# Strassen output product: stores of groups 1 to 7 issued by GpSimd behind its placing of the keys; banks of the x tiles shifted by two

## The chip, the cores and the metric

The kernel runs on one core of a Trainium2 chip. The metric is device time in microseconds, as the median of several executions. A profile is one execution recorded by the hardware profiler; times within it count from the start of its span. The engines are TensorE (PE; its weight loads are listed apart as PEld), VectorE (DVE), ScalarE (ACT), GpSimd (POOL) and SyncE (SP). A name with a small q (ACTq, SPq) is the engine's queue of instructions, where the issue of a transfer shows.

## The reference: what is computed

An attention with pooled keys and values for 8 batches of 8 heads feeds a two-layer block over all 4608 tokens.

```python
# q, k, v: (8, 8, 576, 64) float32
k_p = k.reshape(B, H, 72, 8, D).mean(axis=3)
v_p = v.reshape(B, H, 72, 8, D).mean(axis=3)
scores = matmul(q, k_p.T) / sqrt(D)
attn = softmax(scores)
x = matmul(attn, v_p)                  # -> (4608, 512), one row per token
h = x @ w_in                           # (4608, 2048)
out = (h - tanh(h)) @ w_out            # (4608, 512)
```

The kernel works through the tokens in nine groups of 512 (0 to 8). From group 1 on the last product is made with Strassen's seven half-size products instead of eight.

## The kernel before: the parts that matter here

Each group g from 1 to 8 has two stages. In the hidden stage TensorE computes 16 blocks of h, in seven pairs and two single blocks; ScalarE makes the Tanh and VectorE the difference. In the product stage the seven products run, and between them the attention of batch nb = g + 1 is made, which fills later columns of xT. Meanwhile the keys, values and queries of batch nn = g + 2 are loaded and pooled. Group 6 is the first for which there is no nn, groups 7 and 8 have no nb either.

```python
def h_pair(g, p, b0, ts):
    h_mms(g, p, PS[:, b0, :])                 # line 530: 4 multiplies each
    h_mms(g, p + NP, PS[:, b0 + 1, :])
    t2 = TS[:, 2 * ts : 2 * ts + 2, :]
    nc.scalar.activation(out=t2, in_=PS[:, b0 : b0 + 2, :], func=ACT.Tanh)            # 542
    nc.vector.tensor_sub(out=Gt[:, p, :, :], in0=PS[:, b0 : b0 + 2, :], in1=t2)       # 543
# h_one, lines 547 and 548: the same for one block

def store_tile(g, tb):
    for r0, r1, dst in out_segments(g * TG + tb * 128, 128):
        nc.scalar.dma_start(out=dst, in_=O[r0:r1, tb, :])                             # 607
# out_segments: one piece of 128 rows or two of 64, by where the tile lies in its batch

def after_product(g, n):                      # parts of it
    if n == 0:
        nc.scalar.copy(out=m4, in_=chain(g, C1))                                      # 624
    if n == 1:
        nc.vector.tensor_tensor(out=O[:, 2:4, 0:HD], in0=chain(g, C2), in1=m4, ...)   # 626
        sum_d(0, 2); sum_d(2, 4)                                                      # 561
    if n == 2:
        nc.scalar.copy(out=m45, in_=chain(g, C1))                                     # 630
        nc.gpsimd.tensor_tensor(out=m4, in0=O[:, 2:4, 0:HD], in1=m45, ...)            # 631
        sum_d(4, 6); sum_d(6, 8)
    if n == 3:
        nc.vector.tensor_tensor(out=O[:, 0:2, HD:DM], in0=m4, in1=chain(g, C2), ...)  # 635
    ...                                       # n == 4: 637, 638; n == 5: 640

for g in range(1, NG):
    nb = g + 1 if g + 1 < B else None
    nn = g + 2 if g + 2 < B else None
    for p in range(NP - 1):                   # hidden stage
        c = p if g > 1 else p - 1
        if nb is not None and 0 <= c < 3:
            q_cast_part(nb, c)                # ScalarE, lines 192 and 197
        h_pair(g, p, (0, 2, 4, 6, 0, 2, 4)[p], p % 2)
        ...                                   # sum_p: VectorE, line 551
        if g > 1 and p >= 3:
            store_tile(g - 1, p - 3)
        if nb is not None and p == 0:
            k_dma_transpose(nb)               # SyncE, line 332
            k_place(nb, nc.gpsimd.tensor_copy)   # lines 300, 301, 304
        if nb is not None and 0 <= c < 3:
            q_dma_transpose(nb, 2 * c, min(2 * c + 2, R + 1))   # SyncE, line 205
        if nb is not None and c == 2 and nn is not None:
            load_k(nn); load_v(nn); load_q(nn)   # SyncE, lines 137, 146, 141, 170, 162
    h_one(g, NP - 1, 1, 0, 2)
    h_one(g, NP - 1, 0, 1, 3)
    ...
    ps_a = Banks(2, 3, 4, 5, 0, 1)            # each tile takes the next bank in turn
    for u in range(14):                       # product stage
        n, half = u // 2, u % 2
        product(...)                          # line 586
        if half:
            after_product(g, n)
        if nb is not None:
            if u < NT:                        # NT = 5
                scores(nb, u)                 # two tiles of ps_a; Exp: line 368
            if u in (6, 7, 8, 9, 11):
                av(nb, (6, 7, 8, 9, 11).index(u), ps_b1, True)   # two tiles of ps_a
            if u == 6 and nn is not None:     # lines 248 to 256 and 267 to 291
                pool_k(nn, nc.gpsimd); pool_v(nn, nc.gpsimd)
    if g < NG - 1:
        nc.scalar.copy(out=O[:, 0:2, 0:HD], in_=chain(g, C1))    # line 980
```

The function av multiplies the exponentials with the values (line 396), divides on VectorE (lines 413 and 414, output x_sb) and lets SyncE transpose the result into xT by a transfer (line 434). O is a single buffer of one group's output: it is rewritten in the product stage while its earlier contents were stored in the hidden stage.

Of the kernel before, what the change touches and what calls it, by code (L numbers as in the profile page):

```python
# [28 lines left out]
NT = 5  # L29
# [13 lines left out]
def kernel(  # L43
# [9 lines left out]
    nc = tc.nc  # L53
# [30 lines left out]
    ps_a = Banks(5, 6, 7)  # L84
# [19 lines left out]
    O = const.tile([128, 4, DM], FP32, name="O")  # L104
# [45 lines left out]
    def load_k(b):  # L150
        return [
            load_main(k_pairs, k_raw[b % 2], b, 0, NM),
            load_dense(k_pairs, k_raw[b % 2], b),
        ]

    def load_v(b):
        return [load_main(v_pairs, v_raw[b % 2], b, 0, NM)] + load_left(
            v_pairs, v_raw[b % 2], b
        )
# [29 lines left out]
    def q_cast_part(b, n):  # L189
        t = q_raws[b]  # L190
        if n < 2:
            nc.scalar.copy(
                out=q_bf[:, 2 * n : 2 * n + 2, :, :].rearrange("p j h d -> p h j d"),
                in_=t[:, :, 2 * n : 2 * n + 2, :],
            )
        else:
            nc.scalar.copy(out=q_bf[:QT, R, :, :], in_=q_raws.pop(b)[:QT, :, R, :])

    def q_dma_transpose(b, j0=0, j1=R + 1):
        if j0 == 0:  # L200
            qTs[b] = work.tile([128, NHP, S], BF16, name="qT", tag="qT")
        qT = qTs[b]
        for j in range(j0, j1):
            rows = 128 if j < R else QT
            nc.sync.dma_start_transpose(  # L205
                out=qT[:, :, j * 128 : j * 128 + rows],
                in_=q_bf[:rows, j, :, :].rearrange("p h d -> p (h d)"),
            )
# [89 lines left out]
    def kb_main(kb, ps, t0, t1, engs):  # L298
        kv = kb.rearrange("p (t x) -> p t x", x=KP)
        engs[0](out=kv[0:D, t0:t1, 0:G], in_=ps[0:D, :, 0:G])  # L300
        engs[1](out=kv[D:128, t0:t1, G:128], in_=ps[D:128, :, G:128])

    def kb_left(kb, ps, eng):
        eng(
            out=kb[D:128, :].rearrange("p (t x) -> p t x", x=KP)[:, :, 128 : 128 + LO],
            in_=ps[D:128, 0 : NM * LO].rearrange("p (x t) -> p t x", t=NM),
        )
# [22 lines left out]
    def k_dma_transpose(b):  # L330
        kT = work.tile([128, NT, 128], BF16, name="kT", tag="kT", bufs=1)
        nc.sync.dma_start_transpose(
            out=kT[:, :, :], in_=kdups.pop(b)[:, :, :, :].rearrange("p t a d -> p (t a d)")
        )
        kTs[b] = kT

    def k_place(b, eng):
        kT = kTs.pop(b)
        kb_main(KB[b % 2], kT[:, 0:NM, :], 0, NM, (eng, eng))
        kb_left(KB[b % 2], kT[:, NM, :], eng)  # L340
# [3 lines left out]
    def score_mms(b, t, dst, c0, c1, pairs=range(NM)):  # L344
        for m in pairs if t == NM else (t,):
            o = m * KP + (128 if t == NM else 0)
            w = 32 if t == NM else 128
            p = 32 * m if t == NM else 0
            nc.tensor.matmul(  # L349
                dst[p : p + w],  # L350
                lhsT=KB[b % 2][:, o : o + w],
                rhs=qTs[b][:, m, c0:c1],
                start=True,
                stop=True,
            )

    def scores(b, t):
        if t == 0:
            E_tiles[b] = work.tile([128, NT, S], BF16, name="E", tag="E", bufs=1)
        E = E_tiles[b]  # L360
        hs = S // 2
        pss = []
        for half in range(2):
            ps = ps_b1([128, hs], FP32, "s_ps")
            score_mms(b, t, ps[:, :], half * hs, (half + 1) * hs)
            pss.append(ps)
        for half, ps in enumerate(pss):
            nc.scalar.activation(  # L368
                out=E[:, t, half * hs : (half + 1) * hs], in_=ps[:, :], func=ACT.Exp, scale=SCALE
            )  # L370
# [85 lines left out]
    def out_segments(c0, nrows):  # L456
        segs = []
        r = 0
        while r < nrows:
            c = c0 + r  # L460
            bb = c // S
            i = c % S
            if i < QA:
                j = i // 128
                p0 = i % 128
                ln = min(128 - p0, nrows - r, QA - i)
                dst = out[bb * S : bb * S + QA, :].rearrange("(p j) m -> p j m", j=R)[
                    p0 : p0 + ln, j, :
                ]
            else:  # L470
                ln = min(S - i, nrows - r)
                dst = out[bb * S + i : bb * S + i + ln, :]
            segs.append((r, r + ln, dst))
            r += ln
        return segs
# [62 lines left out]
    def h_pair(g, p, b0, ts):  # L538
        h_mms(g, p, PS[:, b0, :])
        h_mms(g, p + NP, PS[:, b0 + 1, :])  # L540
        t2 = TS[:, 2 * ts : 2 * ts + 2, :]
        nc.scalar.activation(out=t2, in_=PS[:, b0 : b0 + 2, :], func=ACT.Tanh)  # L542
        nc.vector.tensor_sub(out=Gt[:, p, :, :], in0=PS[:, b0 : b0 + 2, :], in1=t2)  # L543
# [6 lines left out]
    def sum_p(a, b):  # L550
        nc.vector.tensor_tensor(  # L551
            out=P[:, a:b, :], in0=Gt[:, a:b, 0, :], in1=Gt[:, a:b, 1, :], op=ALU.add
        )

    def sum_q(a, b):
        nc.vector.tensor_tensor(
            out=Q[:, a:b, :], in0=Gt[:, a:b, 0, 0:HT], in1=Gt[:, a:b, 1, HT:TG], op=ALU.add
        )
# [9 lines left out]
    def w_sum(out, a, b, op, eng=nc.vector, k0=0, k1=NP):  # L568
        return eng.tensor_tensor(  # L569
            out=out[:, k0:k1, :], in0=a[:, k0:k1, :], in1=b[:, k0:k1, :], op=op  # L570
        )
# [32 lines left out]

    def store_tile(g, tb):
        for r0, r1, dst in out_segments(g * TG + tb * 128, 128):
            nc.scalar.dma_start(out=dst, in_=O[r0:r1, tb, :])

    def sh(c, off):
        return slice(c.start + off, c.stop + off)  # L610
# [99 lines left out]
    for m, base, step, cm in (  # L710
# [6 lines left out]
            out=m,  # L717
            in_=m,
# [6 lines left out]
    for i in range(2):  # L725
# [4 lines left out]
        out=spread.rearrange("p (t x) -> p t x", x=32)[:, :, 0:LO],  # L730
        in_=ident[:, 0 : NM * LO].rearrange("p (x t) -> p t x", t=NM),
# [44 lines left out]
    def ps_b1(shape, dtype, name):  # L776
        return ps_a.tile(shape, dtype, name=name, tag="ps_a")
# [110 lines left out]
    for u in range(16):  # L888
        qd, tb = u // 4, u % 4
# [27 lines left out]
        if u in (9, 11):  # L917
            n = (u - 9) // 2
            nc.scalar.mul(
                out=w2s[:, 4, 4 * n : 4 * n + 4, :], in_=b22[:, 4 * n : 4 * n + 4, :], mul=-1.0  # L920
# [10 lines left out]
# [3 lines that stand above are left out]
        for p in range(NP - 1):  # L934
            c = p if g > 1 else p - 1
            if nb is not None and 0 <= c < 3:
                q_cast_part(nb, c)
            h_pair(g, p, (0, 2, 4, 6, 0, 2, 4)[p], p % 2)
            if g == 1 and p < 4:
                w_sum(w2s[:, 0, :, :], b11, b22, ALU.add, k0=2 * p, k1=2 * p + 2)  # L940
            if 3 <= p < 6:
                sum_p(2 * p - 6, 2 * p - 4)
            if g > 1 and p >= 3:
                store_tile(g - 1, p - 3)
            if nb is not None and p == 0:
                k_dma_transpose(nb)
                k_place(nb, nc.gpsimd.tensor_copy)
            if nb is not None and 0 <= c < 3:
                q_dma_transpose(nb, 2 * c, min(2 * c + 2, R + 1))
            if nb is not None and c == 2:  # L950
                if nn is not None:
                    load_k(nn)
                    load_v(nn)
                    load_q(nn)
        h_one(g, NP - 1, 1, 0, 2)
        h_one(g, NP - 1, 0, 1, 3)
        sum_p(6, 8)
        sum_q(0, 4)
        sum_q(4, 8)
        ps_a = Banks(2, 3, 4, 5, 0, 1)  # L960
        for u in range(14):
            n, half = u // 2, u % 2
            bk, lhs, rhs = products[n]
            if n == 6 and g == NG - 1:
                break
            product(g, bk, lhs, rhs, 4 * half, 4 * half + 4, n < 2)
            if half:
                after_product(g, n)
                if g == 1 and n in (1, 2):
                    w_sum(w2s[:, 2, :, :], b21, b22, ALU.add, k0=4 * n - 4, k1=4 * n)  # L970
            if nb is not None:
                if u < NT:
                    scores(nb, u)
                if u in (6, 7, 8, 9, 11):
                    av(nb, (6, 7, 8, 9, 11).index(u), ps_b1, True)
                if u == 6 and nn is not None:
                    pool_k(nn, nc.gpsimd)
                    pool_v(nn, nc.gpsimd)
        if g < NG - 1:
            nc.scalar.copy(out=O[:, 0:2, 0:HD], in_=chain(g, C1))  # L980
# [43 lines left out]
```

## Time and profile before

| | |
|---|---|
| time, median of 3 (range) | 326.88 us (323.62 to 327.22) |
| span of the profiled execution | 324.4 us, 5421 instructions |
| mean granted TensorE clock | 0.963 |
| busy: PE, DVE, ACT, POOL | 287.1, 229.6, 153.0, 122.7 us |
| busy: share of the span | 88%, 71%, 47%, 38% |
| moved by transfers | 49.84 MB, mean 154 GB/s |
| stores by line 607 | 44, from ScalarE: 32 of 128 KB, 12 of 256 KB, median 2.9 us to land |
| weight loads from GpSimd | 8 of 512 KB, median 13.9 and 17.0 us to land |

Busy shares are averages over stages with different limits. The hidden stage and the product stage of one group can have different bounds, and idle time of an engine that nobody waits for costs nothing. What counts is, at each stage, the wait that ends last; the timeline of a stage, beside the same stage of another group, shows it.

### The profile page before, as it was taken

The numbers are of one execution on the slowest core, as the hardware profiler recorded it, in microseconds if no ns is written. First come the engines' busy times: TensorE is split into PE (matmuls) and PEld (weight loads), VectorE is DVE, ScalarE is ACT, GpSimd is POOL, SyncE is SP. The second block draws the span as 40 slices with busy tenths as digits, with TensorE's granted clock in tenths as the row PEclk, the third lists the DMA queues.
The fourth block names the chain that finished last, engine by engine and source line by source line (L and its number), as shares of the span: only waits on it lengthen the run. The fifth ranks groups of instructions, "written<-read, shape, count | busy, mean of one in ns | idle before, by whom it ended". The sixth has DMA issues, their size and how long they took to land.

```text
span 324.4 us, 5421 instructions
## 1 busy us (share of the span) xinstructions
PE 287.1 (88%) x2021; PEld 181.2 (56%) x2040; DVE 229.6 (71%) x400; ACT 153.0 (47%) x244; POOL 122.7 (38%) x122
## 2 busy tenths in 40 slices
PE   7999999989896499989994697949999999999990
PEld 3554455448643277458642484427846864774680
DVE  5668567799864568788783396737969868947950
ACT  4566674754271433763461524545177326415410
POOL 8403649902970029605950069300980100010020
PEclk9999999999999589999999699998999999999998
DMA  8999999677358813787869603697246033101205
GB/s 262 211 236 267 300 271 313 116 238 218 65 105 244 281 43 65 126 240 264 114 143 317 201 16 60 125 316 219 49 104 146 18 58 77 55 2 61 68 2 130
DMA packets 66379, 49.84 MB, mean 154 GB/s; under 512 B 39985, under 2 KB 53297, under 8 KB 66353
## 3 DMA queue, kind: packets, MB, share of 16 engines
q1 hardware_dynamic: 54736, 35.60, 41.8%
q10 hardware_dynamic: 6864, 9.18, 9.9%
q0 software_dynamic: 4752, 4.72, 8.7%
q8 instruction: 16, 0.26, 0.4%
q14 instruction: 11, 0.08, 0.1%
HBM read 36.70 MB, written 9.44 MB: 142 GB/s over the span
## 4 chain that ended last, share of the span: by engine, by line
PE 57%; DMA 17%; DVE 10%; POOL 4%; SPq 3%; ACT 3%; issue 2%; ACTq 1%; DVEq 0%; POOLq 0%
PE PS L586 26%; PE PS L530 21%; DMA k_raw<-in_k_dram 7%; DMA w1b<-in_moe_w_in_dram 4%; DVE Gt L543 4%; PE PS L512 3%; PE PS L396 3%; PE PS L349 3%; DMA v_raw<-in_v_dram 3%; SPq L205 3%; ACT TS L542 2%; DMA qT<-q_bf 2%; DVE x_sb L414 1%; DVE w2s L569 1%; POOL k_raw L248 1%
## 5 line engine op out<-in xcount | busy, mean ns | idle before, releaser
L530 PE MATMUL PS<-xT,w1b 128*128 128x512 bf16 x496 | 111.1, 379 | 5.4 <-DVE x_sb L414 2.5
L543 DVE TENSOR_TENSOR Gt<-PS,TS 128x1024 bf16<-128x1024 f32 x56 | 68.4, 1222 | 46.9 <-ACT TS L542 46.9
L530 PEld LDWEIGHTS <-w1b 128*128 128x128 f16 x512 | 49.7, 98 | 64.2 <-issue 2.8
L542 ACT ACTIVATE TS<-PS 128x1024 f32<-128x1024 f32 x56 | 57.3, 1025 | 53.5 <-PE PS L530 26.6
L631 POOL TENSOR_TENSOR m<-O,m 128x512 f32<-128x512 f32 x8 | 11.5, 1438 | 159.9 <-ACT m L630 125.6
L586 PEld LDWEIGHTS <-Gt 128*128 128x128 bf16 x256 | 23.9, 98 | 28.3 <-DVE Gt L543 17.0
L586 PE MATMUL PS<-w2s,Gt 128*128 128x256 f16 x128 | 19.4, 286 | 20.2 <-DVE Gt L543 15.6
L414 DVE TENSOR_TENSOR x_sb<-PS,rden 128x256 bf16<-128x256 f32 x72 | 30.6, 425 | 2.5
L586 PE MATMUL PS<-w2s,Dg 128*128 128x256 f16 x256 | 30.2, 272 | 0.0
L586 PEld LDWEIGHTS <-P 128*128 128x128 bf16 x256 | 26.4, 105 | 6.7 <-issue 1.4
L248 POOL TENSOR_TENSOR k_raw<-k_raw 128x512 f32<-128x512 f32 (+2 forms) x13 | 22.5, 1746 | 16.3 <-DMA k_raw<-in_k_dram 16.3
L368 ACT ACTIVATE E<-PS 128x288 bf16<-128x288 f32 x60 | 21.4, 412 | 10.8 <-PE PS L349 10.7
L586 PEld LDWEIGHTS <-Dg 128*128 128x128 bf16 x256 | 24.6, 98 | 2.8 <-issue 0.2
L561 DVE TENSOR_TENSOR Dg<-Gt 128x1024 bf16<-128x1024 bf16 x32 | 23.2, 785 | 0.0
L551 DVE TENSOR_TENSOR P<-Gt 128x1024 bf16<-128x1024 bf16 x32 | 22.0, 687 | 0.6
L396 PE MATMUL PS<-VB,E 128*128 128x130 bf16 x240 | 20.2, 220 | 0.1
L586 PE MATMUL PS<-w2b,P 128*128 128x256 f16 x128 | 19.8, 310 | 0.0
L267 POOL TENSOR_TENSOR v_raw<-v_raw 128x512 f32<-128x512 f32 (+1 forms) x12 | 19.2, 1623 | 0.0
L349 PE MATMUL PS<-qT,KB 128*128 128x288 bf16 (+5 forms) x128 | 18.5, 303 | 0.3
L637 ACT COPY m<-PS 128x512 f32<-128x512 f32 x8 | 4.7, 587 | 29.5 <-PE PS L586 29.5
L396 PEld LDWEIGHTS <-E 128*128 128x128 bf16 x240 | 16.8, 98 | 1.9 <-issue 0.4
L586 PE MATMUL PS<-w2s,P 128*128 128x256 f16 x128 | 16.5, 275 | 0.0
(108 smaller groups left out, 371.7 us busy)
## 6 DMA issues: line engine op xcount, KB each, us to landing
k_raw<-in_k_dram SPq DMA_DIRECT2D x7, 1024.0 KB, 6.2
q_raw<-in_q_dram SPq DMA_DIRECT2D x7, 1024.0 KB, 8.2
v_raw<-in_v_dram SPq DMA_DIRECT2D x7, 1024.0 KB, 8.7
out_dram<-O ACTq DMA_DIRECT2D x32, 128.0 KB, 2.9
out_dram<-O ACTq DMA_DIRECT2D x12, 256.0 KB, 2.9
w1b<-in_moe_w_in_dram POOLq DMA_DIRECT2D x4, 512.0 KB, 13.9
w2b<-in_moe_w_out_dram POOLq DMA_DIRECT2D x4, 512.0 KB, 17.0
out_dram<-O SPq DMA_DIRECT2D x4, 256.0 KB, 5.0
```

What stands on the lines that cost most here:

```text
L248: first = eng.tensor_tensor(out=r[:, ta:tb, 0:4, :], in0=r[:, ta:tb, 0:4, :], in1=r[:, ta:tb, 4:8, :], op=ALU.add)
L267: eng.tensor_tensor(out=r[:, ta:tb, 0:4, :], in0=r[:, ta:tb, 0:4, :], in1=r[:, ta:tb, 4:8, :], op=ALU.add)
L349: nc.tensor.matmul(dst[p : p + w], lhsT=KB[b % 2][:, o : o + w], rhs=qTs[b][:, m, c0:c1], start=True, stop=True,)
L368: nc.scalar.activation(out=E[:, t, half * hs : (half + 1) * hs], in_=ps[:, :], func=ACT.Exp, scale=SCALE)
L396: nc.tensor.matmul(ps[:, 2 * n : 2 * n + 2, :].rearrange("p h d -> p (h d)") if n < 2 else ps.rearrange("p (a s) d -> p a s d", s=2)[:, :, ...
L414: nc.vector.tensor_tensor(out=x_sb[:, half, :, :], in0=ps[:, :, 0:D], in1=rden[:, :, :].to_broadcast([128, 4, D]), op=ALU.mult,)
L530: nc.tensor.matmul(dst, lhsT=w1b[:, fb, i * 128 : (i + 1) * 128], rhs=xT[:, fb, c0 : c0 + TG], start=(fb == 0), stop=(fb == NFB - 1),)
L542: nc.scalar.activation(out=t2, in_=PS[:, b0 : b0 + 2, :], func=ACT.Tanh)
L543: nc.vector.tensor_sub(out=Gt[:, p, :, :], in0=PS[:, b0 : b0 + 2, :], in1=t2)
L551: nc.vector.tensor_tensor(out=P[:, a:b, :], in0=Gt[:, a:b, 0, :], in1=Gt[:, a:b, 1, :], op=ALU.add)
L561: nc.vector.tensor_tensor(out=Dg[:, a:b, :, :], in0=Gt[:, a:b, :, 0:HT], in1=Gt[:, a:b, :, HT:TG], op=ALU.subtract,)
L586: nc.tensor.matmul(part(g, bk, tt), lhsT=lhs(k, slice(tt * 128, (tt + 1) * 128)), rhs=rhs[:, k, :], start=(first and k == 0 and (tt == 0 o ...
```

## The change

The stores of groups 1 to 7 (line 607) are issued by GpSimd instead of ScalarE, and no longer one tile after each of the hidden pairs 3 to 6 but all four tiles after the first pair, behind the placing of the keys in GpSimd's queue. The purpose is to keep store issues out of ScalarE's queue, in which the Tanh stands, without holding up the placing. Where a following batch exists, the rotation of ps_a is also advanced by two tiles between the scores and the x tiles, so that the x tiles use other banks of PSUM.

```diff
     def store_tile(g, tb):
         for r0, r1, dst in out_segments(g * TG + tb * 128, 128):
-            nc.scalar.dma_start(out=dst, in_=O[r0:r1, tb, :])
+            nc.gpsimd.dma_start(out=dst, in_=O[r0:r1, tb, :])
...
             if 3 <= p < 6:
                 sum_p(2 * p - 6, 2 * p - 4)
-            if g > 1 and p >= 3:
-                store_tile(g - 1, p - 3)
             if nb is not None and p == 0:
                 k_dma_transpose(nb)
                 k_place(nb, nc.gpsimd.tensor_copy)
+            if g > 1 and p == 0:
+                for tb in range(4):
+                    store_tile(g - 1, tb)
...
                 if u < NT:
                     scores(nb, u)
+                if u == NT:
+                    ps_a.n += 2
                 if u in (6, 7, 8, 9, 11):
                     av(nb, (6, 7, 8, 9, 11).index(u), ps_b1, True)
```

The other stores stay as they were: group 0's tiles are stored by SyncE (line 525), and group 8's by SyncE and ScalarE (lines 603 and 993).

## The prediction

> **What bounds the kernel now.** I began with the summary by engine and the chain that ended last. TensorE is busy 88% of the 324.4 us span and carries 57% of the chain; but a further 17% of the chain is transfers, and the largest of these is a load of keys (7%), which no matrix multiply of that moment needs. So I read the same stage of several groups in the timeline. A group has two stages: the hidden layer (line 530, its Tanh at line 542, its subtraction at line 543) and the Strassen products (line 586). The rows below are columns of start, duration, engine, instruction, and in brackets the idle time before it and what ended it. Group 2:
>
> ```profile
> 98.53 1.17 ACTq L607 DMA_DIRECT2D out_dram<-O  x2
> 98.83 0.57 SPq L137 DMA_DIRECT2D k_raw<-in_k_dram  x1
> 99.80 1.02 ACT L542 ACTIVATE TS<-PS 128x1024 f32<-128x1024 f32 x1 [2.78 <-PE PS L530]
> 105.25 1.12 ACTq L607 DMA_DIRECT2D out_dram<-O  x2
> 106.48 1.02 ACT L542 ACTIVATE TS<-PS 128x1024 f32<-128x1024 f32 x1 [5.65 <-DMA k_raw<-in_k_dram]
> 107.53 1.23 DVE L543 TENSOR_TENSOR Gt<-PS,TS 128x1024 bf16<-128x1024 f32 x1 [4.72 <-ACT TS L542]
> 108.81 0.61 PE L586 MATMUL PS<-w2s,Gt 128*128 128x256 f16 x2 [5.84 <-DVE Gt L543]
> 109.34 1.08 ACT L547 ACTIVATE TS<-PS 128x512 f32<-128x512 f32 x2 [1.83 <-DMA out_dram<-O]
> ```
>
> ScalarE sits idle 5.65 us in front of a Tanh, and what ended the wait is a load of keys that Tanh doesn't read. The store of output ahead of it in ScalarE's own queue was held; it cannot issue before the key load has landed, VectorE waits for the Tanh (4.72 us) and TensorE for VectorE (5.84 us). The chain of waits tells it in order:
>
> ```profile
> 99.45 6.29 DMA k_raw<-in_k_dram
> 105.77 0.61 ACTq L607
> 106.50 2.84 DMA out_dram<-O
> 109.35 0.60 ACT TS L547
> ```
>
> Why a store waits for a load is in the instruction lists of the built program: transfers of SyncE and ScalarE are counted on eight shared completion counters handed out in turn over both engines, and each transfer waits for the previous one on its counter. In group 2 the third output tile's store drew the counter of the key load.
>
> Group 6 has the same stores and the same attention for the following batch, but no loads (batch 8 does not exist). The windows of the hidden stage (columns: window, length, busy us and instructions of PE, PEld, DVE, ACT, POOL, PE clock, DMA share, GB/s), groups 2, 4, 5, 6:
>
> ```profile
> 87.16:110.72 23.56, 16.21 (x79) 7.67 (x81) 12.31 (x17) 10.60 (x14) 7.79 (x9) 0.90 0.69 188
> 158.60:181.80 23.20, 16.02 (x78) 7.63 (x80) 12.37 (x17) 10.71 (x14) 7.88 (x9) 0.91 0.78 210
> 198.80:219.00 20.20, 15.51 (x77) 7.52 (x80) 10.45 (x11) 9.84 (x13) 6.49 (x8) 0.99 0.72 194
> 234.90:248.40 13.50, 13.43 (x62) 6.17 (x63) 10.33 (x13) 10.11 (x12) 7.55 (x9) 1.00 0.61 137
> ```
>
> In group 6 TensorE is busy 13.43 of 13.50 us; in groups 2, 4 and 5 the stage is 7 to 10 us longer though the work is equal. From the first line-530 multiply of one group to that of the next (87.16, 127.11, 158.59, 198.77, 234.49, 263.70) groups 2 to 6 take 39.95, 31.48, 40.18, 35.72 and 29.21 us.
>
> **What the Trainium skill says.** "DMA: Bandwidth & Descriptors", section "Issuing engines are not separate DMA queues": transfers of all issuers run on the same 16 engines, so a new issuer saves only the issuing engine's time. The trace agrees for the bandwidth: group 3's last two stores, issued beside the key and value loads, took 7.6 us to land against medians of 2.3 to 2.7 us in groups 6 to 8, where no load runs. The time saved here is large only because the issuing queue also waits. The same page, "SWDGE vs HWDGE vs iDMA": GpSimd makes its descriptors in software and writes them to SBUF. Before, its eight weight loads cost it 746 to 782 ns each; I use 0.75 us a store, though no run shows that for a store. "SBUF — State Buffer", section "Who interferes with whom": a VectorE instruction with two SBUF inputs contends with a GpSimd one that reads SBUF. The trace agrees: line 561 takes 952 ns in group 3's product stage, beside pooling, and 683 ns in group 6's, which has none.
>
> **The change part by part.** Removed: 44 store issues from ScalarE, 0.34 to 0.86 us each, median 0.48. In group 6 none of them delays a Tanh (the waits there are 0.54 to 0.70 us for TensorE), so the issue time itself is worth nothing. What counts is the waiting in groups 2 to 5. The changed program's lists show GpSimd's stores on counters of their own; no store waits for a load, and SyncE's loads no longer wait for stores. If groups 2 to 5 then ran like group 6: 147.33 us now (39.95 + 31.48 + 40.18 + 35.72) less 4 x 29.21 = 116.84 leaves 30.5 us. That is the ceiling.
>
> Added: 5 to 8 stores per group on GpSimd, 3.75 to 6.0 us, behind the key placing. GpSimd runs pooling of keys (3.0 to 3.5 + 1.54 + 1.87), of values (3.03 + 1.55 + 0.86 + 1.04 + 0.62) and the placing (1.0) without a break after line 631, which in group 6 begins 21.4 us into the group. 1.4 + 6.7 + 7.1 + 1.0 = 16.2 us later it is free: 37.6 us, or 8.4 us into the next group of 29.2. The stores are issued from 8.4 to 12 or 14.4 us into the group. They must have landed before line 626 overwrites O, at 18.3 us in group 6 (252.78 less 234.49). With 2.9 us to land (the median before), there are 1 to 3 us to spare; but loads start about 11.7 us into the group, and the last stores, tiles 2 and 3, are the ones that line 626 waits for. At 7.6 us to land the last arrives at about 20 to 22 us, and line 626 is 2 to 3.5 us late. Part of that is absorbed: in group 3 before, it started at 147.92, 20.8 us into the group, after 1.36 us on a store, and TensorE's next dependent product still ran at 149.02.
>
> Moved: the x tiles. Before, the last three of a group (u = 8, 9, 11) lie in banks 4-5, 0-1, 2-3, and the next group's first hidden pair writes 0-1. Groups 4 and 5 opened with waits on line 414 of 0.69 and 1.76 us:
>
> ```profile
> 198.77 13.97 PE L530 MATMUL PS<-xT,w1b 128*128 128x512 bf16 x62 [1.76 <-DVE x_sb L414]
> ```
>
> After, they lie in 0-1, 2-3, 4-5, in the order in which the pairs want them, and these waits go. They are inside the 30.5 us, so nothing is added. The cost: attention's first x tile waits for the fourth score tile's Exp instead of the third's, which is over by then.
>
> Against the ceiling I set 1.0 us per group: VectorE beside pooling (line 561 four times 0.27 us more, line 638 1.26 instead of 0.69), the late line 626, and transposes of x sharing DMA with the earlier query load. Sum: 30.5 - 4 x 1.0 = 26.5 us; 326.88 - 26.5 = 300.4.
>
> **Rivals.** First, the GpSimd ring: line 631, pooling, placing, stores, landing, line 626, and line 631 again. It takes 1.5 + 6.9 + 7.1 + 1.0 + 6.0 + 2.9 + 0.7 = 26.1 us with quick landing, below 29.2 and so harmless; with a landing of 7.6 it is 30.8, and with stores of 1.1 us too some 33. At 31 to 32 us per group the saving falls to about 20 to 23: 304 to 307. For it: GpSimd has no gap from line 631 to placing. Against it: the first stores leave before the loads start. Second, DMA as the bound: loads, stores and transposes squeezed into 29 us. Group 3 ran at 31.48 with all of it and 2.3 us of ScalarE idle in front of one Tanh, so this costs at most about 2 us a group: 305 to 308. Third, the waits come from transfers simply being slow and reappear elsewhere, on q or x: then 315 to 325. Against it: a key load lands in 6.3 us and the product stage that needs it begins later.
>
> **Range and chances.** The low end is the full ceiling, 326.9 - 30.5 = 296.4, with a run-to-run us; the high end is the first rival with slow stores. Slower would need stores to block GpSimd for more than the 30 us that the waits cost. Predicted 300.4 us, 8 in 10 between 295.5 and 309; faster by over 2% 0.93, within 2% 0.05, slower by over 2% 0.02.
>
> **What would show it.** Right: no Tanh of groups 2 to 5 waits on a transfer; hidden stages of 13.5 to 14.5 us; groups of 29 to 31 us; first hidden multiplies not released by line 414. The steps in doubt show as waits of line 626 on a store, as the time of one store on GpSimd, and as the placing's time into the group. I am wrong if GpSimd's stores take well over 1 us each, or if placing comes so late that the scores at the start of the product stage wait for it.

## The result and the profile after

| | before | after |
|---|---|---|
| time, median of 4 executions (range) | 326.73 us (323.62 to 327.22) | 302.14 us (300.66 to 307.02) |
| ratio, 95% interval | | 0.9247 [0.9175, 0.9319] |
| groups 2 to 6 in a profile | 39.95, 31.48, 40.18, 35.72, 29.21 us | 31.42, 29.86, 32.67, 29.22, 29.74 us |
| TensorE busy, mean granted clock | 287.1 us, 0.963 | 280.3 us, 0.992 |
| GpSimd busy | 122.7 us | 144.0 us |

The prediction was 300.4 us with a range of 295.5 to 309; the result lies 1.7 us above the prediction. The profile shown of after is of the same kernel measured once more, with a span of 301.2 us (the first run below). The profile of the first measurement is of its slowest execution (305.3 us); groups 2 to 6 took 31.50, 31.12, 32.20, 30.88 and 31.40 us in it.

The windows of the hidden stage after, groups 2, 4, 5 and 6, with the columns of the windows shown before (window, length, busy us and instructions of PE, PEld, DVE, ACT, POOL, clock, DMA share, GB/s):

```profile
87.41:101.30 13.89, 13.89 (x65) 6.35 (x66) 10.54 (x15) 9.70 (x11) 11.98 (x17) 1.00 0.61 127
148.69:162.60 13.91, 13.91 (x67) 6.34 (x66) 10.71 (x15) 10.52 (x12) 11.59 (x16) 1.00 0.62 133
181.36:195.30 13.94, 13.94 (x66) 6.38 (x67) 9.42 (x10) 8.99 (x10) 7.81 (x13) 1.00 0.74 164
210.58:224.50 13.92, 13.92 (x68) 6.34 (x65) 10.74 (x15) 10.52 (x12) 11.13 (x16) 1.00 0.60 138
```

TensorE is busy from end to end in every one of them. The windows of groups 2, 4 and 5 before were longer by 7 to 10 us, but not all of that was waiting: they also took in 15 to 17 multiplies of the products and scores (77 to 79 instructions in all, against 62 in group 6). The hidden multiplies of group 2 ended at 101.14 us before, 13.98 us into the group, just as after; the waits came behind them. TensorE waited 5.84 + 1.29, 4.17 + 2.94 and 4.59 us there. In the waits of the whole execution before (engine and tile, line, what ended the wait: us in total, times, longest) these make up most of the first two rows, and the Tanhs' waits for transfers are the other three:

```profile
PE PS L586 <- DVE Gt L543: 15.6, 5, 5.8
PE PS L586 <- DVE Gt L548: 4.6, 4, 2.9
ACT TS L542 <- DMA k_raw<-in_k_dram: 10.1, 2, 5.7
ACT TS L542 <- DMA out_dram<-O: 5.2, 1, 5.2
ACT TS L547 <- DMA out_dram<-O: 1.8, 1, 1.8
```

After, the first two are 0.2 us each and the other three are gone. The timeline of group 2 after (start, duration, engine, instruction, and in brackets the idle time before it and what ended it) shows why, and shows what came in their place:

```profile
95.43 4.25 POOL L607 DMA_DIRECT2D out_dram<-O  x8
97.98 1.02 ACT L542 ACTIVATE TS<-PS 128x1024 f32<-128x1024 f32 x1 [0.70 <-PE PS L530]
99.35 1.02 SPq L137 DMA_DIRECT2D k_raw<-in_k_dram  x1
99.71 1.02 ACT L542 ACTIVATE TS<-PS 128x1024 f32<-128x1024 f32 x1 [0.70 <-PE PS L530]
103.86 0.28 PE L349 MATMUL PS<-qT,KB 128*128 128x288 bf16 x1 [1.47 <-DMA qT<-q_bf]
```

The Tanhs of pairs 3 to 6 now wait 0.70 us each, for TensorE, as in group 6 before, although the key load goes out between two of them. The last line is new: a score multiply (line 349) of the product stage waits for a transpose of queries. The waits of the whole execution after have two rows on TensorE's multiplies that a transfer ended:

```profile
PE PS L530 <- DMA xT<-x_sb: 4.6, 3, 3.3
PE PS L349 <- DMA qT<-q_bf: 2.2, 3, 1.5
```

(The expectations below count the waits of TensorE's weight loads too, 1.1 and 1.4 us, and so speak of 5.7 and 3.6 us.) Of the 4.6 us, 0.9 stood at the start of group 2 before too. The remaining 3.7, 3.29 of it at the start of group 5, and the 2.2 make 5.9 us. A clean group takes 29.22 us (shown below), so groups 2 to 6 are 2.20 + 0.64 + 3.45 + 0 + 0.52 = 6.8 us longer than they could be, and these two rows are most of it. How they divide changes from one execution to another: in the profile of the first measurement they are 3.7 us for x and 5.4 us for the queries.

### The profile page after: what moved, and what is told of

Read it like the earlier page. It is cut to its first block, busy times and chain, and to the rows that moved or that the text cites. A ratio compares the mean times of both kernels' runs of the same rounds, so it can differ in the third digit from the quotient of the medians.

```text
span 305.3 us, 5447 instructions
## 1 busy us (share of the span) xinstructions
PE 280.5 (92%) x2021; PEld 178.8 (59%) x2040; DVE 229.7 (75%) x400; ACT 154.0 (50%) x244; POOL 143.8 (47%) x166
## 4 chain that ended last, share of the span: by engine, by line
PE 62%; DMA 20%; DVE 6%; POOL 4%; SPq 2%; issue 2%; ACT 1%; ACTq 0%; POOLq 0%; DVEq 0%
PE PS L530 27%; PE PS L586 24%; DMA qT<-q_bf 7%; DMA w1b<-in_moe_w_in_dram 4%; PE PS L512 4%; DMA k_raw<-in_k_dram 4%; DMA xT<-x_sb 3%; PE PS L396 3%; PE PS L349 3%; DVE Gt L543 3%; DMA v_raw<-in_v_dram 2%; POOL k_raw L248 1%; DVE w2s L569 1%; SPq L137 1%; SPq L141 1%
## 5 line engine op out<-in xcount | busy, mean ns | idle before, releaser
L530 PE MATMUL PS<-xT,w1b 128*128 128x512 bf16 x496 | 112.7, 383 | 5.7 <-DMA xT<-x_sb 3.7
L631 POOL TENSOR_TENSOR m<-O,m 128x512 f32<-128x512 f32 x8 | 10.5, 1309 | 105.2 <-DVE Dg L561 60.2
L586 PE MATMUL PS<-w2s,Dg 128*128 128x256 f16 x256 | 30.2, 273 | 0.0
L607 POOL DMA_DIRECT2D out_dram<-O x44 | 23.6, 546 | 13.4 <-ACT O L983 13.4
L248 POOL TENSOR_TENSOR k_raw<-k_raw 128x512 f32<-128x512 f32 (+2 forms) x13 | 21.5, 1674 | 17.2 <-DMA k_raw<-in_k_dram 17.2
L586 PEld LDWEIGHTS <-P 128*128 128x128 bf16 x256 | 24.6, 98 | 4.7 <-issue 1.4
L349 PE MATMUL PS<-qT,KB 128*128 128x288 bf16 (+5 forms) x128 | 17.5, 290 | 5.6 <-DMA qT<-q_bf 5.4
L561 DVE TENSOR_TENSOR Dg<-Gt 128x1024 bf16<-128x1024 bf16 x32 | 22.1, 751 | 0.0
L396 PE MATMUL PS<-VB,E 128*128 128x130 bf16 x240 | 20.2, 221 | 0.1
L586 PE MATMUL PS<-w2s,Gt 128*128 128x256 f16 x128 | 16.7, 273 | 0.4 <-DVE Gt L548 0.2
L413 DVE RECIPROCAL rden<-PS 128x4 f32<-128x4 f32 x72 | 12.5, 174 | 5.5 <-PE PS L396 5.5
```

The source lines that it names most:

```text
L248: first = eng.tensor_tensor(out=r[:, ta:tb, 0:4, :], in0=r[:, ta:tb, 0:4, :], in1=r[:, ta:tb, 4:8, :], op=ALU.add)
L349: nc.tensor.matmul(dst[p : p + w], lhsT=KB[b % 2][:, o : o + w], rhs=qTs[b][:, m, c0:c1], start=True, stop=True,)
L396: nc.tensor.matmul(ps[:, 2 * n : 2 * n + 2, :].rearrange("p h d -> p (h d)") if n < 2 else ps.rearrange("p (a s) d -> p a s d", s=2)[:, :, ...
L530: nc.tensor.matmul(dst, lhsT=w1b[:, fb, i * 128 : (i + 1) * 128], rhs=xT[:, fb, c0 : c0 + TG], start=(fb == 0), stop=(fb == NFB - 1),)
L561: nc.vector.tensor_tensor(out=Dg[:, a:b, :, :], in0=Gt[:, a:b, :, 0:HT], in1=Gt[:, a:b, :, HT:TG], op=ALU.subtract,)
L586: nc.tensor.matmul(part(g, bk, tt), lhsT=lhs(k, slice(tt * 128, (tt + 1) * 128)), rhs=rhs[:, k, :], start=(first and k == 0 and (tt == 0 o ...
```

## The experiments

Every time is a median over all executions of a run. Every ratio is to the kernel before on the same chip and leaves out executions over 1.5% above the fastest of their kernel (two of the four with the loads behind the stores, whose 0.9194 therefore stands for about 300 us beside the median of 302.89). Group lengths come from one profile each, from the first line-530 multiply of a group to that of the next, so that a wait at a group's start counts to the group before it.

| experiment | us | ratio, 95% | groups 2 to 6, us |
|---|---|---|---|
| after, again | 302.0 | 0.9237 [0.9164, 0.931] | 31.42, 29.86, 32.67, 29.22, 29.74 |
| stores only | 302.25 | 0.9267 [0.9196, 0.9338] | 31.84, 29.38, 31.44, 29.21, 29.22 |
| shift only | 326.26 | 1.0015 [0.9986, 1.0043] | 39.30, 32.71, 39.22, 36.72, 29.22 |
| loads behind stores | 302.89 | 0.9194 [0.9101, 0.9287] | 32.70, 31.11, 31.95, 30.90, 29.22 |
| no stores | 295.7 | 0.9044 [0.8973, 0.9115] | 29.23, 29.22, 29.22, 29.22, 29.22 |
| early stores | 302.43 | 0.9244 [0.9171, 0.9317] | 31.16, 29.75, 30.72, 30.16, 30.40 |
| early key load | 311.61 | 0.9509 [0.9409, 0.961] | 33.77, 35.55, 33.04, 31.33, 30.41 |
| both early | 306.38 | 0.9374 [0.9309, 0.9438] | 31.28, 33.35, 30.69, 30.92, 29.62 |
| staggered stores | 316.73 | 0.9701 [0.9637, 0.9765] | 35.15, 33.90, 36.26, 34.46, 29.22 |
| pooling ahead | 317.09 | 0.9708 [0.9662, 0.9753] | 33.19, 33.95, 32.39, 30.74, 31.04 |
| ScalarE best | 299.55 | 0.9191 [0.9136, 0.9246] | 30.69, 30.49, 29.21, 29.22, 29.22 |
| ScalarE best, again | 299.17 | 0.9144 [0.9103, 0.9185] | 30.88, 30.30, 30.12, 29.37, 29.23 |

**The changed kernel again, unedited.** It gave the profile above.

> The changed kernel once more, beside the other kernels of this series and on their chip. Theory and rival both expect the 302.1 us of the first measurement within 1%, with groups 2 to 6 each taking 31 to 31.5 us from first hidden multiply to first hidden multiply, and TensorE waiting at line 349 (scores) for transposes of queries in several groups. If the group that began late because of a transpose of x (group 5, 2.8 us) was a disturbance of that one execution, it is gone here.

Measured: 302.0 us. The wait for x at the start of group 5 was not a thing of one execution, as the expectation allowed: it is there again, with 3.29 us after 2.8 us in the first profile.

**Either half alone.** Stores only:

```diff
                 if u < NT:
                     scores(nb, u)
-                if u == NT:
-                    ps_a.n += 2
```

> Stores on GpSimd behind the placing, x tiles in their old banks. Theory (the stores carry the gain): 302 to 305 us, at most 1% slower than the whole change, with waits of line 530 on line 414 of 0.5 to 2 us at the starts of groups 3 to 5. Rival (the bank shift carries an appreciable part): 308 us or more.

Shift only, with the stores on ScalarE as before:

```diff
-            nc.gpsimd.dma_start(out=dst, in_=O[r0:r1, tb, :])
+            nc.scalar.dma_start(out=dst, in_=O[r0:r1, tb, :])
...
+            if g > 1 and p >= 3:
+                store_tile(g - 1, p - 3)
...
-            if g > 1 and p == 0:
-                for tb in range(4):
-                    store_tile(g - 1, tb)
```

> Only the banks shifted, stores as before from ScalarE. Theory: 324 to 327 us, within 1% of before, because the Tanh of groups 2, 4 and 5 still waits on key loads and the stall swallows what the shift gives. Rival (the shift is worth something by itself): 320 us or less.

The stores bring the whole gain, and the shift nothing that can be measured: 302.25 beside 302.0 us, and 1.0015 [0.9986, 1.0043] over 20 executions. The shift alone does shorten the waits of line 530 for line 414, from 2.5 us to 0.3, but the Tanhs wait for transfers as before (10.6 us for the key load, 7.7 us for stores) and the time stays. The waits of 0.5 to 2 us on line 414 that the first expectation looked for in stores only did not come: line 530 never waits for line 414 there, without the shift as well.

**Does the store's engine matter, or the load ahead of it?** This one keeps the stores on ScalarE behind pairs 3 to 6 as before, leaves out the shift, and lets the three loads go out only behind the Tanh of pair 6 (`after` makes a transfer wait for an instruction; h_pair returns its Tanh as `th`):

```diff
-        nc.scalar.activation(out=t2, in_=PS[:, b0 : b0 + 2, :], func=ACT.Tanh)
+        th = nc.scalar.activation(out=t2, in_=PS[:, b0 : b0 + 2, :], func=ACT.Tanh)
...
-            if nb is not None and c == 2:
-                if nn is not None:
-                    load_k(nn)
-                    load_v(nn)
-                    load_q(nn)
+        if nn is not None:
+            after(load_k(nn), th)
+            load_v(nn)
+            load_q(nn)
```

> Stores stay on ScalarE, one tile after each of pairs 3 to 6, with their 44 issues; the loads of the batch after next are held until the Tanh of the last pair, so that in the instruction lists the stores draw counters last used by transposes and not by loads. Banks as before. Theory (what cost the time was the wait for a load on a shared counter, not ScalarE's issuing): 302 to 309 us, no Tanh waits for a load. Rival (issuing from ScalarE is itself the cost, or transfers are slow and the wait moves): 316 us or more.

Its timeline in group 2, in an execution of 305.43 us (line 608 is before's 607):

```profile
97.82 1.93 ACTq L608 DMA_DIRECT2D out_dram<-O  x2
99.85 1.02 ACT L542 ACTIVATE TS<-PS 128x1024 f32<-128x1024 f32 x1 [1.01 <-PE PS L530]
100.88 1.12 ACTq L608 DMA_DIRECT2D out_dram<-O  x2
101.33 0.40 SPq L137 DMA_DIRECT2D k_raw<-in_k_dram  x1
```

The stores stand in ScalarE's queue as before, each ahead of a Tanh, and no Tanh waits for a transfer. The time is 302.89 us. So it is not the issuing of stores on ScalarE that cost 24 us, but the loads ahead of them. The link between the two is the completion counter, and the kept traces record it for each transfer. Before, the transfers of SyncE and ScalarE use the same eight counters, and those of GpSimd eight others. In group 2 the store that goes out at 105.25 us is on the counter of the key load, which had gone out at 98.83 us and landed at 105.23; the store at 108.71 us is on that of a value load, which landed at 108.69. In the run with the loads behind the stores, the counters of group 2's stores were last used by transposes and earlier stores. No run changed the counters alone. The loads now go out about 2 us later in the group (14.1 us instead of 11.7 before and 11.9 after). The landing of x transposes ends 4.4 us of waits of line 530, about as after (4.6 us), and line 414 ends another 1.7 us.

**The ceiling.** The 44 stores of groups 1 to 7 are left out, so that the output rows of these groups are never written; the rest is after's:

```diff
-            if g > 1 and p == 0:
-                for tb in range(4):
-                    store_tile(g - 1, tb)
```

> The changed kernel with the 44 stores of groups 1 to 7 left out (this output is not written). Theory (what is left over the ceiling is transfers of the same core competing: stores with the transposes of queries, loads with those of x): waits of TensorE on the transposes of queries (3.6 us in the repeat of the changed kernel) fall below 0.5 us, those on transposes of x (5.7 us) fall to 2 to 4 us as the loads end earlier, time 296 to 299 us. Rival (the residue is VectorE beside pooling, or TensorE's clock): time stays within 1% of 302, waits move to VectorE.

Measured: 295.7 us, 30.4 below the kernel before on that chip, and every group takes 29.22 or 29.23 us. Loads, pooling, placing and all transposes fit into 29.22 us. What stands between after and this ceiling, 302.1 - 295.7 = 6.4 us, comes with the stores. The run takes away their transfers and GpSimd's issuing (44 x 0.54 = 24 us) together; that in after TensorE waits for transposes in groups 2 to 6, and never for GpSimd, speaks for the transfers. SyncE's queue shows how they reach the x transposes. After, group 4 (start 148.69):

```profile
165.42 0.47 SPq L170 DMA_DIRECT2D q_raw<-in_q_dram  x1
168.93 0.63 SPq L162 DMA_DIRECT2D q_raw<-in_q_dram  x1
171.71 10.70 SPq L434 DMA_TRANSPOSE xT<-x_sb  x6
```

The same three rows without stores, group 4 (start 145.75):

```profile
160.10 0.47 SPq L170 DMA_DIRECT2D q_raw<-in_q_dram  x1
162.07 0.63 SPq L162 DMA_DIRECT2D q_raw<-in_q_dram  x1
168.78 9.44 SPq L434 DMA_TRANSPOSE xT<-x_sb  x6
```

The x transposes start 23.0 us into the group in both. But the last part of the query load goes out 20.2 us into the group instead of 16.3. Of these 3.9 us, 2.4 have passed by line 170 already, most of them because the seven issues from the key load on took 6.0 us instead of 3.8. The other 1.5 us pass in front of line 162, where SyncE's queue waits for the key load to land. It is the counters again: line 162 is the ninth transfer of SyncE from the key load on and takes up the key load's counter (the load lands at 168.91 us, line 162 goes out at 168.93). In the whole execution these waits are 13.8 us in six, against 8.6 without stores, and key loads of the middle groups take 9.0 us to land instead of 5.8. The query load therefore flows for longer while the x transposes run: it lands 6.2 us after the first of them goes out, instead of 2.5. The chain of waits shows the decisive one landing after 6.71 us. The median of an x transpose is 2.5 to 2.7 us.

**Stores earlier.** If the burst delays the query transposes, it should leave sooner. GpSimd makes only the first step of the value pooling, then issues the stores, then places the keys and finishes the pooling:

```diff
     def pool_v(b, eng):
+        pool_v_first(b, eng)        # line 267 alone
+        return pool_v_rest(b, eng)
...
             if nb is not None and p == 0:
                 k_dma_transpose(nb)
-                k_place(nb, nc.gpsimd.tensor_copy)
             if g > 1 and p == 0:
                 for tb in range(4):
                     store_tile(g - 1, tb)
+            if nb is not None and p == 0:
+                k_place(nb, nc.gpsimd.tensor_copy)
+                if g > 1:
+                    pool_v_rest(nb, nc.gpsimd)
...
-                    pool_v(nn, nc.gpsimd)
+                    pool_v_first(nn, nc.gpsimd)
```

> All stores written, but GpSimd issues them after the first step of value pooling, ahead of the placing and of the rest of the pooling, some 4 to 5 us earlier in the group, before the transposes of queries. Theory: waits on transposes of queries below 1.5 us, those on transposes of x unchanged at 4 to 6 us, time 299 to 302 us. Rival (earlier stores collide with key and query transposes all the same and the placing comes too late): 302 us or more, with scores waiting for the placing on GpSimd.

The stores leave 2.8 us into group 3, no score waits for qT any more, and the waits for xT are down to the 0.9 us that stood at the start of group 2 before. The time is 302.43 us all the same. Its timeline in group 6 (start 209.18):

```profile
220.21 1.54 DVE L558 TENSOR_TENSOR P<-Gt 128x1024 bf16<-128x1024 bf16 x1
221.28 1.20 POOL L280 TENSOR_TENSOR v_raw<-v_raw 128x320 f32<-128x320 f32 x1
222.56 1.04 POOL L288 TENSOR_TENSOR VB<-v_raw,mask 128x512 bf16<-128x512 f32 x1
222.92 1.23 DVE L558 TENSOR_TENSOR P<-Gt 128x1024 bf16<-128x1024 bf16 x1
```

VectorE's sums (line 558 here, 551 before) take 1.54 and 1.23 us beside the pooling instead of 0.69, VectorE is busy 236.0 us instead of 229.9, and the multiplies of the products wait for VectorE (2.8 and 1.2 us on its lines 550 and 555, before's 543 and 548). What was gained on the transfers was lost on VectorE.

**Key load earlier.** The key load goes out behind the key transpose, ahead of the query transposes, so that the loads are done before the x transposes:

```diff
             if nb is not None and p == 0:
                 k_dma_transpose(nb)
+                if g > 1 and nn is not None:
+                    load_k(nn)
...
                 if nn is not None:
-                    load_k(nn)
+                    if g == 1:
+                        load_k(nn)
```

> The changed kernel with the load of keys, from group 2 on, issued behind the transpose of keys and ahead of the transposes of queries, some 7 to 8 us earlier; values and queries as before. Theory (the transposes of x wait behind the query load on the same queue): waits of line 530 on transposes of x fall from 5.7 to under 2.5 us, but those on transposes of queries rise (3.6 to 4 to 7 us), since the key load now lies ahead of them; time 299 to 303 us. Rival (transposes of x are late for another reason): their waits stay at 4 to 6 us and the time rises to 304 us or more.

The combination with the early stores has both edits:

> Early stores and early key load together. Theory: both waits small (x under 2.5 us, queries under 3 us in total), 297 to 300 us, better than the changed kernel. Rival: stores, key load and query transposes crowd the first half of the hidden stage, and the queries' transposes come later than before: 302 us or more.

Two rows of the waits of the early key load alone:

```profile
PE PS L349 <- DMA qT<-q_bf: 12.3, 5, 4.7
PE PS L530 <- DMA xT<-x_sb: 0.9, 1, 0.9
```

The x side is cured as intended, but the load now runs under the query transposes: their median landing rises to 5.6 us from 2.5, and the scores wait 12.3 us in five times. 311.61 us is well above what was expected. Both early gives 306.38 us instead of the 297 to 300 hoped for: the scores still wait 4.6 us, the placing waits 9.3 us for the key transposes, and the VectorE cost of early stores is there (235.6 us busy).

**Stores spread out.** GpSimd's stores are each held until the Tanh of pairs 3 to 6, where ScalarE issued them before:

```diff
-            if g > 1 and p == 0:
-                for tb in range(4):
-                    store_tile(g - 1, tb)
+            if g > 1 and p >= 3:
+                after(store_tile(g - 1, p - 3), th)
```

> The changed kernel, but GpSimd's store of each tile is held until the Tanh of pair 3, 4, 5 or 6, as ScalarE's stores were, so the stores are spread over some 6 us instead of 3 to 4. Theory (stores in one burst hold up the transposes of queries): waits on those transposes fall from 3.6 to under 1 us; but the last stores now land beside the loads, so the waits on transposes of x stay at 4 to 8 us; 300 to 303 us. Rival (spreading does not matter): both waits as in the changed kernel, 301 to 303 us, or line 626 waits on a store, over 303 us.

It took 316.73 us, far above the expectation. The stores go out beside the loads, as before, yet no Tanh waits for a transfer; issuing them from GpSimd is enough for that, without the earlier time. The waits on transposes are down to 0.3 us (queries) and 1.1 us (x). But TensorE now waits for VectorE (lines 587, 629, 562 and 634 are before's 586, 626, 561 and 631):

```profile
PE PS L396 <- DVE x_sb L414: 8.9, 8, 2.0
PE PS L587 <- DVE O L629: 4.8, 4, 2.3
```

Group 2 in its timeline (start 87.79):

```profile
109.40 0.69 DVE L629 TENSOR_TENSOR O<-PS,m 128x512 f32<-128x512 f32 x1 [3.76 <-DMA out_dram<-O]
110.01 6.24 DVE L562 TENSOR_TENSOR Dg<-Gt 128x1024 bf16<-128x1024 bf16 x4
110.27 1.55 POOL L634 TENSOR_TENSOR m<-O,m 128x512 f32<-128x512 f32 x1 [7.82 <-DVE O L629]
111.78 3.92 POOL L248 TENSOR_TENSOR k_raw<-k_raw 128x512 f32<-128x512 f32 x2
```

The same in after, group 2 (start 87.41):

```profile
107.34 0.69 DVE L626 TENSOR_TENSOR O<-PS,m 128x512 f32<-128x512 f32 x1 [2.09 <-ACT E L368]
107.95 2.48 DVE L561 TENSOR_TENSOR Dg<-Gt 128x1024 bf16<-128x1024 bf16 x4
110.47 1.26 POOL L631 TENSOR_TENSOR m<-O,m 128x512 f32<-128x512 f32 x1 [10.78 <-DVE Dg L561]
```

Line 626 waits for a store that left late and starts 21.6 us into the group instead of 19.9. That is 1.7 us, but in after GpSimd's addition began just when the four Dg sums were over (it had waited for the copy of line 630, done at 110.34). Now both run side by side, the sums take 6.24 us instead of 2.48, VectorE's divisions of the x tiles (line 414) come late, TensorE waits for them, and the Dg product starts 30.2 us into the group (117.99) instead of 27.0 (114.42). The Trainium skill, "SBUF — State Buffer", section "Who interferes with whom", states the rule: a VectorE instruction with two SBUF inputs and a GpSimd one that reads SBUF contend. This run agrees and adds the size: a Dg sum takes 0.68 us alone, and each of the twelve that ran wholly beside a GpSimd addition took 1.75 to 2.29 us.

**Pooling ahead.** The first step of the key pooling is put ahead of line 631, to have GpSimd free sooner:

```diff
+                if u == 4 and nn is not None:
+                    pool_k(nn, nc.gpsimd, step=1)      # line 248 alone
                 if u == 6 and nn is not None:
-                    pool_k(nn, nc.gpsimd)
+                    pool_k(nn, nc.gpsimd, step=2)      # the rest
```

> The changed kernel, but the first step of key pooling (3.1 us) runs on GpSimd ahead of line 631 instead of behind it, so that placing and stores come 3 us earlier without moving pooling beside the P sums of VectorE. Theory: waits on transposes of queries under 2.5 us and of x under 4 us, 298 to 301 us. Rival: the key load has not landed by then, line 631 and behind it line 635 are late, TensorE waits for VectorE, 302 us or more.

317.09 us: the same collision by another way. Its timeline in group 3 (lines 249 and 564 are before's 248 and 561):

```profile
145.63 3.48 POOL L249 TENSOR_TENSOR k_raw<-k_raw 128x512 f32<-128x512 f32 x2 [10.41 <-DMA k_raw<-in_k_dram]
145.90 7.38 DVE L564 TENSOR_TENSOR Dg<-Gt 128x1024 bf16<-128x1024 bf16 x4
```

GpSimd stands 10.41 us in front of the key load and then begins 0.3 us ahead of the Dg sums, which take 7.38 us. VectorE is busy 247.2 us in all, the most of any run. As the rival of the expectation had it, the key load has not landed by then. Group 1, which the table leaves out, suffers most: 36.98 us instead of 31.30, with one wait of 4.29 us of TensorE for VectorE's x_sb.

**ScalarE best.** From these a version follows that needs no GpSimd: stores on ScalarE one pair earlier, behind pairs 2 to 5, all loads held until the Tanh of pair 5, and the shift. Against before:

```diff
-            if g > 1 and p >= 3:
-                store_tile(g - 1, p - 3)
+            if g > 1 and 2 <= p < 6:
+                store_tile(g - 1, p - 2)
+            if nn is not None and p == 5:
+                after(load_k(nn), th)
+                load_v(nn)
+                load_q(nn)
...
-            if nb is not None and c == 2:
-                if nn is not None:
-                    load_k(nn)
-                    load_v(nn)
-                    load_q(nn)
```

> Stores on ScalarE, one tile after each of pairs 2 to 5, loads held until the Tanh of pair 5, banks shifted as in the change. Theory: as good as the change or better, 299 to 302 us, waits on transposes of queries under 1 us, those of x 3 to 6 us (7.5 us where loads were held longer). Rival (ScalarE's issue time counts once the waits are gone): 303 us or more, with Tanh late for TensorE.

> The version with stores on ScalarE, loads held until the Tanh of pair 5 and banks shifted, once more with more repetitions, to narrow its ratio to the kernel before. Theory (ScalarE is as good an issuer as GpSimd once no load is ahead on the counter): 298.5 to 301 us, ratio 0.913 to 0.922, that is at or slightly below the changed kernel's 0.924. Rival (its 299.6 us was a lucky draw and ScalarE's issue time counts): 302 us or more, ratio 0.926 or above.

It gave 299.55 and 299.17 us, 0.9191 [0.9136, 0.9246] and 0.9144 [0.9103, 0.9185]. Its groups 4 to 6 run at 29.2 us in the first profile, the ceiling, and at 30.12, 29.37 and 29.23 in the second. It is about 2.7 us (0.9%) below after, beside after's own 0.9247 [0.9175, 0.9319] and 0.9237 [0.9164, 0.931]. The intervals of these comparisons touch or overlap, so that a gain over after is likely but small. From the run with the loads behind the stores (0.9194 [0.9101, 0.9287]) it differs in three things, one pair earlier, the loads behind pair 5, and the shift; by the ratios no gain from them is shown. It is not free of the old wait: in its two profiles one and two Tanhs wait for a store, 1.1 and 3.2 us in all.

## Why the prediction was right, and where it was off

- **What bounds the kernel: right.** No Tanh of after waits for a transfer, while the kernel before had 17.1 us of such waits (10.1 on the key load, 7.0 on stores). The run with the loads behind the stores reaches the same time with the stores still on ScalarE, and the shift alone changes nothing.
- **The windows: misread.** "The work is equal" does not hold for them (79 and 62 instructions), and of the 7 to 10 us only 7.1, 7.1 and 4.6 us were TensorE's waits. The ceiling was taken from whole groups, which do hold equal work, and so did not suffer.
- **The ceiling of 30.5 us: right.** The step "if groups 2 to 5 then ran like group 6" gave 296.4 us; without stores the kernel takes 295.7. Part of it is clock, which the prediction does not name: TensorE's mean granted clock was 0.87, 0.92 and 0.95 in groups 2, 4 and 5 before and 1.00 in each after, and with the same multiplies its busy time in groups 2 to 5 falls from 124.5 to 117.6 us. The step took this in because group 6, its yardstick, ran at 1.00.
- **Stores on GpSimd: mis-sized, to the good side.** 0.75 us a store was taken from the weight loads; a store took 0.53 to 0.60 us, median 0.544. They are issued 8.0 to 12.3 us into group 2, where 8.4 to 14.4 was predicted, and land in 4.0 us (median; at most 6.0).
- **Line 626 "2 to 3.5 us late": did not come.** In after it never waits for a store. Quicker stores landed in time: the last of group 2 lands 17.0 us into the group, and line 626 starts at 19.9. The staggered stores show what a later landing does.
- **The shift: right.** It adds nothing to the stores.
- **The residue, 4 x 1.0 us: this step failed.** It measured 6.4 us and consists in part of other things, so that the sum came within 1.7 us is partly luck; groups 2 and 4, at 31.42 and 32.67 us, lie outside the 29 to 31 us that it gave as the sign of being right. It was put down to VectorE beside pooling, the late line 626, and x transposes sharing DMA with the query load. The reading behind the first was not exact: of group 3's four Dg sums before, three took 0.68 to 0.69 us and one 1.76, and that one ran mostly beside line 631, not beside pooling. Only the third cost is there (3.7 us of waits beyond before's), and in a sharper form: the stores slow the loads, and the last query load is held back on SyncE until the key load has landed. What was missing is the query transposes, which are issued in the same stretch as GpSimd's burst (2.2 us). The late line 626 and VectorE beside pooling cost nothing that shows in after; the two variants in which GpSimd's additions met the Dg sums are some 15 us slower than after.
- **Group 6 as untouched: wrong, by 0.5 us in this profile.** It has stores but no loads, and took 29.74 us instead of 29.21: one of its score multiplies waits 0.35 us for qT.
- **The rivals.** The second, DMA, was close to the truth: its "at most about 2 us a group" compares with 6.8 us over five groups. The third, waits reappearing on q and x, happened with 6 us over the ceiling, where its 315 to 325 us mean 19 to 29. The first, the GpSimd ring through line 626, stays out of after and is what the staggered stores ran into, at 316.7 instead of its 304 to 307: it counted line 626's delay, which ends 4.8 us of TensorE's waits, and not the collision with the Dg sums that follows from it, behind which stand 8.9 us.

## What to carry to other kernels

When an engine waits for a transfer whose data it doesn't read, look at the issue that stands in front of it in its own queue and at what that issue waits for; the two can be tied together by nothing but a completion counter. Then either the issue or the transfer it waits for can be moved, and here both cures gave about the same time. Take the ceiling from a stage of the same kernel that lacks the cause, and a run without the moved transfers tells how much of the rest is theirs. Before shifting work on GpSimd by a few us, see which VectorE sums it will then run beside.

## What had not been expected of the hardware

- Transposes by transfer suffer under a competing load: with the 1 MB key load ahead of them, the query transposes' median landing went from 2.5 to 5.6 us (longest 9.7).
- Four bf16 sums on VectorE with both inputs in SBUF took 2.48 us alone, and 6.24 to 7.38 us beside GpSimd additions; a delay of 1.7 us in one instruction was enough to bring it about.
- The issue of a store took GpSimd 0.54 us, less than its weight loads (746 to 782 ns). The Trainium skill, "DMA: Bandwidth & Descriptors", section "Issuing engines are not separate DMA queues", says that another issuer saves only the issue time, which is usually small. The equal times of stores on GpSimd (302.0 us) and of stores on ScalarE ahead of the loads (302.9 us) agree with that: the 24 us came from stores waiting for loads, not from the time ScalarE spent on issuing.
